# Adjacent weight rows per partition, d(o) as rows on four column groups, and four output buffers in a decode layer's forward and backward

## The chip, the cores and the metric

The kernel runs on one core of a Trainium2 chip. The metric is the device time of one execution in microseconds, the median of several runs. The time before is 290.5 us (five runs, 288.19 to 291.11 us).

## The reference

One decode step of a parallel layer: with `xn = layernorm(x)`, the output is `x + attention(xn) + ffn(xn)`, and all gradients for a given `grad_out` are returned too. There are 4 batch rows of one token, D = 512, 32 query heads in 8 key/value groups, head size 128, a cache of 4096 positions of which the last 1024 are attended, and a feed-forward width of 1792. Everything is bfloat16.

```python
def _A_ref(x, k_cache, v_cache, wq, wo):      # Hq 32, Hkv 8, Dh 128, W = 1024, rep = 4
    q = (x @ wq).reshape(B, Sq, Hq, Dh).transpose(0, 2, 1, 3)
    k = jnp.repeat(k_cache[:, :, Sk - W:, :], rep, axis=1)
    v = jnp.repeat(v_cache[:, :, Sk - W:, :], rep, axis=1)
    p = softmax(einsum("bhqd,bhkd->bhqk", q, k) * Dh ** -0.5)
    o = einsum("bhqk,bhkd->bhqd", p, v)
    return o.transpose(0, 2, 1, 3).reshape(B, Sq, Hq * Dh) @ wo

def _B_ref(x, w_gate, w_up, w_down):
    return (gelu(x @ w_gate) * (x @ w_up)) @ w_down

xn = layernorm(x)
out = x + _A_ref(xn, ...) + _B_ref(xn, ...)
# returned: out, and the gradients to x, k_cache, v_cache, wq, wo, w_gate, w_up, w_down
```

The gradients to the caches are 4 x 8 x 4096 x 128 each. They are zero outside the attended 1024 positions, and these zeros have to be written too: 50 MB of the 81 MB that the kernel writes.

## The kernel before

**Start and feed-forward.** x and grad_out are loaded with every batch row repeated on 32 partitions (`x_b`, `dy_b`, lines 110 to 114). The three feed-forward weights, the first two groups' wo and wq and most of their k and v are loaded on SP's queue. A weight matrix of 512 rows lies on 128 partitions as four chunks: partition p holds rows p, 128 + p, 256 + p and 384 + p (lines 118 to 122, 222), so each row is one contiguous run. `wo` has 1024 rows to a head group, laid out likewise as eight chunks of 128 rows of 1 KB (line 221). `xnT` and `dyT` (lines 204 to 210) are the normalized x and the gradient with D on the partitions, in the same chunk order. `xnm` and `dym` (lines 213 to 218) hold the rows masked by `msk_i`, so that partition b*32 + i keeps only row i of its block of 32: an outer product with a tile that has head i on that partition picks this head.

The feed-forward part (lines 516 to 659) transposes weights on TensorE (PE), evacuates them with `evac` (line 84) and multiplies them. `evac` gives a PSUM tile to ScalarE (ACT, line 92) or VectorE (DVE, line 94) by an estimate of the load on each; 16-bit tiles go to DVE. The weight gradients are appended as pieces to a list `bg`, and `tick(n)` runs n of them between other matmuls.

**Attention.** Eight key/value groups are taken two at a time, so t runs over 4 head groups of 8 heads each. For each t:

- `pre(t)` (line 280): wo is transposed (line 288), d(o) = wo dy is formed by matmuls of 4 columns (line 293) and q = wq xn likewise (line 298), both into one PSUM tile `doq_ps`. They are copied to `doT` and `qsT` (lines 305 and 307), from there into the zero-padded operands `dom` and `qm` (line 308; two sets, by the parity of t), and transposed to rows `r4` (line 313).
- `masks` (line 318), `scores` (line 327; k for q, then v for d(o), transposed block by block at line 336 and multiplied at line 341 in four column groups of 32), `softmax`, `softmax_d`.
- `odq(t, 0)` and `odq(t, 1)` (line 408): o = p v and dq = ds k, copied from PSUM to rows (lines 421 and 423), which two transposes (line 426) turn into columns (line 428).
- `pre(t + 1)` stands between the two `odq`.
- `fin(t)` (line 497): the products with wo and with the transposed wq are added into `acc`.
- `load_next(t)` (line 242): the loads for t + 2.
- `dw(t)` (line 455) appends the pieces of d(wo) (`piece_o`, line 463) and d(wq) (`piece_q`, line 478); `dvdk` appends those of the cache gradients (line 444).

**Order and queues.** SP issues all loads, in the program's order (`manual_schedule` for that engine alone); the other engines' instructions are placed by a scheduler that keeps to the data flow. GpSimd (POOL) issues the result stores through `store` (line 98). The zeros go out on ACT's queue at fixed points of the program (`zeros(n)`, line 253): each is tied behind the last ACT evacuation recorded then. At the end everything left of the zeros is issued (line 689).

**Pools.** Results wait for their store in `osb_*` tiles from the pool `outp` (line 75, three buffers, 4 KB to a partition) and `stg_*` tiles from `stage` (line 662, three buffers, 8 KB). Each t fills four osb tiles (two `osb_o`, two `osb_q`) and four stg tiles. `stage` and the tiles of odd groups (`wodd`) take the memory that the feed-forward pools gave back (line 661).

**The end** (lines 692 to 721): `acc` is transposed, and the layer norm's backward runs on DVE on 128 x 512 tiles.

Of the kernel before, what the change touches and what calls it, by code (L numbers as in the profile page):

```python
# [14 lines left out]
P = 128  # L15
# [3 lines left out]
def kernel(  # L19
# [23 lines left out]

    nc = tc.nc
# [21 lines left out]
    assert Sq == 1 and Dh == P and D == 512 and F % P == 0 and RG == 32 and JQ * NQ == J and WQ == JQ * P  # L66
# [8 lines left out]
    outp = ctx.enter_context(tc.tile_pool(name="outp", bufs=3))  # L75
# [44 lines left out]
    nc.sync.dma_start(out=wg_sb[:], in_=B_w_gate.rearrange("(c p) f -> p c f", p=P))  # L120
    wu_sb = ffn_w.tile([P, ND, F], BF16, name="wu_sb")
    nc.sync.dma_start(out=wu_sb[:], in_=B_w_up.rearrange("(c p) f -> p c f", p=P))
# [39 lines left out]
    qm_all, dom_all = [], []  # L162
    for i in range(2):
        for lst, nm in ((qm_all, "qm"), (dom_all, "dom")):
            t_ = const.tile([P, NS, RG + rep], BF16, name=f"{nm}{i}")
            nc.gpsimd.memset(t_[:], 0.0)
            lst.append(t_)
# [38 lines left out]
    for src, dstT in ((dy_b, dyT), (xn_b, xnT)):  # L206
        tps = ps_x.tile([P, ND, P], BF16, name="tps", tag="x")
        for c in range(ND):
            nc.tensor.transpose(tps[:, c, :], src[:, c * P:(c + 1) * P], ident[:])
        nc.vector.tensor_copy(out=dstT[:], in_=tps[:].rearrange("p c (b r) -> p c b r", b=B)[:, :, :, 0])  # L210


    xnm = const.tile([P, rep, D], BF16, name="xnm")
    dym = const.tile([P, rep, D], BF16, name="dym")
# [6 lines left out]
    wo_v = A_wo.rearrange("(t h p) n -> t p h n", p=P, h=HG)  # L221
    wq_v = A_wq.rearrange("(c p) (t j) -> t p c j", p=P, j=CW)
# [50 lines left out]
    def tick(n):  # L273
        for _ in range(min(n, len(bg))):
            bg.popleft()()
# [4 lines left out]
    def pre(t):  # L280

        wo_sb, wq_sb = wo_t[t], wq_t[t]
        dq_ps = ps_x.tile([P, 2, HG, B], FP32, name="doq_ps", tag="x")
        for h2 in range(HG // 2):
# [6 lines left out]
            for i in range(2):  # L291
                for c in range(ND):
                    nc.tensor.matmul(dq_ps[:, 0, 2 * h2 + i, :], lhsT=woT[:, i, c, :], rhs=dyT[:, c, :],
                                     start=(c == 0), stop=(c == ND - 1))
            tick(2)
        for h in range(HG):
            for c in range(ND):
                nc.tensor.matmul(dq_ps[:, 1, h, :], lhsT=wq_sb[:, c, h * Dh:(h + 1) * Dh], rhs=xnT[:, c, :],
                                 start=(c == 0), stop=(c == ND - 1))
        T4 = []  # L300
# [451 lines left out]
```

## Time and profile before

| | |
|---|---|
| median of 5 runs | 290.5 us (288.19 to 291.11) |
| profiled execution: its own time / its span | 288.19 us / 286.5 us |
| busy: PE, DVE, ACT, POOL | 207.5, 144.8, 113.8, 66.9 us (72, 51, 40, 23% of the span) |
| mean granted TensorE clock | 0.85 |
| memory traffic | 112.4 MB, mean 392 GB/s; read 30.93 MB, written 81.01 MB |
| landing times (median): wo, wq, kb, vb loads | 10.1, 16.1, 20.0, 48.8 us |
| landing times (median): stg_dv, stg_dk, osb_o, osb_q stores | 10.0, 9.4, 14.1, 12.6 us |
| landing times (median): zeros of 3 MB, of 1.5 MB | 16.4, 15.5 us |

The span runs from the first to the last instruction on the core, and the execution's own time is 1.7 us longer. The page divides the span into 40 equal slices; a digit is the busy share of a slice in tenths. An instruction's "mean ns of one" is its latency; matmuls overlap, so a row of them takes less than their sum. "Idle before" is the time that an engine stood still ahead of such instructions, with what released it. The three busy DMA queues are q1 (SP's loads), q10 (ACT's, here the zeros) and q0 (GpSimd's stores).

### The profile page before, as it was taken

To read this page: it belongs to the slowest core of one execution; us is meant where nothing else is said; L and a number is where in the kernel's file an instruction comes from. 1 tells how busy PE (TensorE), PEld (TensorE's weight loads), DVE (VectorE), ACT (ScalarE), POOL (GpSimd) and SP (SyncE) were. 2 spreads that over 40 slices of the span, in tenths; PEclk is the share of its full clock that TensorE was granted. 3 is DMA by queue.
4 is the path that set the end of the run, shared out by engine and by line. 5 is a ranking of instruction groups with operands and counts; after the bars stand their busy time and mean duration, and the time that the engine had idled before them with its cause. 6 is when DMAs were issued, how large, how long until landed. Compare 5 with 4: busy or idle time off the path is not lost.

```text
span 286.5 us, 6811 instructions
## 1 busy us (share of the span) xinstructions
PE 207.5 (72%) x2946; PEld 142.1 (50%) x2956; DVE 144.8 (51%) x310; ACT 113.8 (40%) x217; POOL 66.9 (23%) x84
## 2 busy tenths in 40 slices
PE   1397994973977899556699987576898688596810
PEld 0386882652644765333357655343575365362310
DVE  5484672333564567313636763145375535455770
ACT  1201654443442467313325653043455444245610
POOL 7000130431303152311033322112162231302410
PEclk9996999597897889795959996959799979869775
DMA  6999999999999999999999999999999999999897
GB/s 169 385 386 380 386 400 419 413 404 431 431 415 431 412 373 388 432 416 422 421 421 344 316 410 423 423 424 418 424 411 396 392 392 414 411 407 377 305 387 287
DMA packets 30181, 112.38 MB, mean 392 GB/s; under 512 B 1536, under 2 KB 7688, under 8 KB 26056
## 3 DMA queue, kind: packets, MB, share of 16 engines
q10 hardware_dynamic: 4612, 50.46, 42.0%
q1 hardware_dynamic: 17732, 30.81, 29.5%
q0 software_dynamic: 7808, 30.67, 27.4%
q8 instruction: 23, 0.38, 0.5%
q14 instruction: 6, 0.05, 0.0%
HBM read 30.93 MB, written 81.01 MB: 391 GB/s over the span
## 4 chain that ended last, share of the span: by engine, by line
PE 47%; DMA 28%; DVE 14%; issue 4%; ACT 3%; POOL 1%; SPq 0%; DVEq 0%; ACTq 0%; POOLq 0%
DMA out_dram<-osb_o 14%; PE T_ps L336 9%; PE kv_ps L444 7%; DMA out_dram<-stg_dv 5%; PE S_ps L341 4%; DVE T_sb L94 4%; DMA wd_sb<-in_B_w_down_dram 4%; PE od_ps L416 3%; DMA out_dram<-osb_d 3%; PE woT_ps L288 3%; PE acc_ps L181 2%; DMA out_dram<-osb_g 2%; PE wgT_ps L648 2%; PE wqT_ps L508 2%; PE dwo_ps L463 2%
## 5 line engine op out<-in xcount | busy, mean ns | idle before, releaser
L94 DVE COPY T_sb<-T_ps 128x1024 bf16<-128x1024 bf16 x64 | 44.2, 691 | 34.7 <-PE T_ps L336 34.3
L92 ACT CAST stg_dv<-kv_ps 128x512 bf16<-128x512 f32 x52 | 28.8, 589 | 43.9 <-PE kv_ps L444 40.9
L92 ACT CAST stg_dk<-kv_ps 128x512 bf16<-128x512 f32 x46 | 25.0, 588 | 15.4 <-PE kv_ps L444 7.6
L336 PE MATMUL T_ps<-ident,vb 128*128 128x128 bf16 x256 | 26.8, 255 | 4.8 <-DVE osb_q L94 4.8
L336 PEld LDWEIGHTS <-vb 128*128 128x128 bf16 x256 | 20.6, 116 | 11.1 <-issue 7.2
L336 PE MATMUL T_ps<-ident,kb 128*128 128x128 bf16 x256 | 24.4, 228 | 0.6 <-ACT stg_dk L92 0.2
L336 PEld LDWEIGHTS <-kb 128*128 128x128 bf16 x256 | 18.2, 102 | 12.3 <-issue 4.9
L92 ACT CAST osb_q<-dwq_ps 128x512 bf16<-128x512 f32 x25 | 13.5, 589 | 27.1 <-DMA out_dram<-osb_o 17.1
L444 PE MATMUL kv_ps<-domr,P_q 128*128 128x512 bf16 x63 | 23.7, 435 | 0.2 <-issue 0.2
L92 ACT CAST osb_g<-dwg_ps 128x384 bf16<-128x384 f32 (+1 forms) x30 | 14.5, 534 | 17.6 <-PE dwg_ps L621 6.4
L444 PE MATMUL kv_ps<-qmr,dS_q 128*128 128x512 bf16 x59 | 18.7, 391 | 3.2 <-ACT stg_dk L92 2.4
L94 DVE COPY woT<-woT_ps 128x1024 bf16<-128x1024 bf16 x16 | 11.1, 692 | 17.9 <-PE woT_ps L288 17.9
L478 PE MATMUL dwq_ps<-od_r,xnm 128*128 128x256 bf16 x64 | 13.1, 334 | 6.0 <-DVE osb_q L94 5.8
L92 ACT CAST osb_o<-dwo_ps 128x512 bf16<-128x512 f32 x23 | 12.8, 588 | 7.8 <-PE dwo_ps L463 7.8
L352 POOL TENSOR_TENSOR dS_q<-dS_b,qmsk 128x1024 bf16<-128x1024 bf16 x4 | 7.5, 1884 | 35.3 <-DVE dS_b L405 35.3
L94 DVE CAST stg_dk<-kv_ps 128x512 bf16<-128x512 f32 x18 | 12.0, 685 | 3.5 <-DMA out_dram<-stg_dv 2.5
L341 PE MATMUL S_ps<-T_sb,dom 128*32 128x256 bf16 x128 | 10.5, 312 | 4.4 <-DVE T_sb L94 4.3
L98 POOL DMA_DIRECT2D out_dram<-stg_dv x8 | 6.2, 774 | 30.9 <-ACT stg_dv L92 30.9
L98 POOL DMA_DIRECT2D out_dram<-osb_q x8 | 5.9, 732 | 31.4 <-ACT osb_q L92 31.3
L94 DVE COPY wqT<-wqT_ps 128x1024 bf16<-128x1024 bf16 x16 | 11.0, 688 | 4.2 <-PE wqT_ps L508 3.9
L288 PE MATMUL woT_ps<-ident,wo_sb 128*128 128x128 bf16 x128 | 12.2, 246 | 0.7 <-ACT osb_g L92 0.5
L94 DVE COPY wgT<-wgT_ps 128x1024 bf16<-128x1024 bf16 x14 | 9.7, 692 | 5.4 <-PE wgT_ps L648 5.4
(187 smaller groups left out, 374.3 us busy)
## 6 DMA issues: line engine op xcount, KB each, us to landing
out_dram<-ztile ACTq DMA_DIRECT2D x8, 3072.0 KB, 16.4
out_dram<-ztile ACTq DMA_DIRECT2D x16, 1536.0 KB, 15.5
kb<-in_A_k_cache_dram SPq DMA_DIRECT2D x8, 1024.0 KB, 20.0
vb<-in_A_v_cache_dram SPq DMA_DIRECT2D x8, 1024.0 KB, 48.8
out_dram<-stg_dv POOLq DMA_DIRECT2D x8, 1024.0 KB, 10.0
out_dram<-stg_dk POOLq DMA_DIRECT2D x8, 1024.0 KB, 9.4
wo_sb<-in_A_wo_dram SPq DMA_DIRECT2D x4, 1024.0 KB, 10.1
wq_sb<-in_A_wq_dram SPq DMA_DIRECT2D x4, 1024.0 KB, 16.1
```

Of the source, the lines that this page charges most:

```text
L92: last.append(nc.scalar.copy(out=out, in_=in_))
L94: return nc.vector.tensor_copy(out=out, in_=in_)
L98: d = eng.dma_start(out=out, in_=in_)
L181: nc.tensor.matmul(ps[:, c, :], lhsT=lf(c), rhs=rhs, start=(k == 0), stop=(k == len(terms) - 1))
L288: nc.tensor.transpose(wT_ps[:, i, c, :], wo_sb[:, 2 * h2 + i, c * P:(c + 1) * P], ident[:])
L336: nc.tensor.transpose(T_ps[:, j, :], blks[(t, g)][:, b, j, :], ident[:])
L341: nc.tensor.matmul(ps[q * RG:(q + 1) * RG, :], lhsT=lf[:, s * RG:(s + 1) * RG], rhs=T_sb[:, q * WQ:(q + 1) * WQ], start=(g == 0 and b == 0 ...
L352: nc.gpsimd.tensor_tensor(out=dst[:], in0=src[:].unsqueeze(1).broadcast_to([P, NQ, WQ]), in1=qmsk[:].unsqueeze(2).broadcast_to([P, NQ, WQ] ...
L416: nc.tensor.matmul(od_ps[b * RB:b * RB + rep, k, g, :], lhsT=pT[:, jj, c0:c0 + rep], rhs=blks[(t, g)][:, b, j, :], start=(j == 0), stop=(j ...
L444: nc.tensor.matmul(mps[:].rearrange("p b d -> p (b d)"), lhsT=src[:, q, jj * P:(jj + 1) * P], rhs=mr[:, g].rearrange("p b d -> p (b d)"), ...
L463: nc.tensor.matmul(mps[:], lhsT=o_r[:, g, :], rhs=dym[:, i, :], start=True, stop=True)
L478: nc.tensor.matmul(mps[:, i].rearrange("p g d -> p (g d)"), lhsT=xnm[:, i2 * 2 + i, c * P:(c + 1) * P], rhs=dq_r[:].rearrange("p g d -> p ...
```

## The change

- The weights' rows are dealt to the partitions in runs of adjacent rows: partition p of a head group's wo holds rows 8p to 8p + 7, and of w_gate, w_up and wq rows 4p to 4p + 3. w_down keeps its layout. The gradients d(wo), d(wq), d(w_gate) and d(w_up) are stored in the same order, xn is transposed with a stride of 4 to match, and the final layer-norm steps read `acc` in that order.
- d(o) is formed as rows: the transposed wo is the moving operand, dy with 8 copies of each batch row (`dyT8`) the stationary one, on four column groups. One copy (`do_row`) and two transposes give the columns back. q keeps its way, in a tile of its own.
- `odq(t, 0)` writes o four times, once per masked head (`o_x`), in the order of the new rows; eight small matmuls with `qmsk` give the columns `oT`, and `piece_o` multiplies `o_x` with `dy_b`. `dym` is then needed by the feed-forward alone and moves to its pool.
- One set of `qm` and `dom` in place of two; four buffers in `outp` in place of three.

```diff
-    outp = ctx.enter_context(tc.tile_pool(name="outp", bufs=3))
+    outp = ctx.enter_context(tc.tile_pool(name="outp", bufs=4))
...
-    nc.sync.dma_start(out=wg_sb[:], in_=B_w_gate.rearrange("(c p) f -> p c f", p=P))
+    nc.sync.dma_start(out=wg_sb[:], in_=B_w_gate.rearrange("(p c) f -> p c f", p=P))
...
-    nc.sync.dma_start(out=wu_sb[:], in_=B_w_up.rearrange("(c p) f -> p c f", p=P))
+    nc.sync.dma_start(out=wu_sb[:], in_=B_w_up.rearrange("(p c) f -> p c f", p=P))
...
-    qm_all, dom_all = [], []
-    for i in range(2):
-        for lst, nm in ((qm_all, "qm"), (dom_all, "dom")):
-            t_ = const.tile([P, NS, RG + rep], BF16, name=f"{nm}{i}")
-            nc.gpsimd.memset(t_[:], 0.0)
-            lst.append(t_)
+    qm, dom = [const.tile([P, NS, RG + rep], BF16, name=nm) for nm in ("qm", "dom")]
+    for t_ in (qm, dom):
+        nc.gpsimd.memset(t_[:], 0.0)
...
-            nc.tensor.transpose(tps[:, c, :], src[:, c * P:(c + 1) * P], ident[:])
+            nc.tensor.transpose(tps[:, c, :], src[:, c:D:ND] if adj else src[:, c * P:(c + 1) * P], ident[:])
...
+            dyT8 = const.tile([P, ND, B * 8], BF16, name="dyT8")
+            nc.vector.tensor_copy(out=dyT8[:].rearrange("p c (b r) -> p c b r", b=B),
+                                  in_=tps[:].rearrange("p c (b r) -> p c b r", b=B)[:, :, :, 0:8])
...
-    dym = const.tile([P, rep, D], BF16, name="dym")
+    dym = ffn.tile([P, rep, D], BF16, name="dym")
...
-    wo_v = A_wo.rearrange("(t h p) n -> t p h n", p=P, h=HG)
-    wq_v = A_wq.rearrange("(c p) (t j) -> t p c j", p=P, j=CW)
+    wo_v = A_wo.rearrange("(t p k) n -> t p k n", p=P, k=HG)
+    wq_v = A_wq.rearrange("(p c) (t j) -> t p c j", p=P, j=CW)
...
     def pre(t):
-        dq_ps = ps_x.tile([P, 2, HG, B], FP32, name="doq_ps", tag="x")
+        E = P // HG
+        do_ps = ps_x.tile([P, HG, GP, E], FP32, name="do_ps", tag="x")
...
-            for i in range(2):
-                for c in range(ND):
-                    nc.tensor.matmul(dq_ps[:, 0, 2 * h2 + i, :], lhsT=woT[:, i, c, :], rhs=dyT[:, c, :],
-                                     start=(c == 0), stop=(c == ND - 1))
+            for c in range(ND):
+                for i in range(rep):
+                    nc.tensor.matmul(do_ps[i * RG:(i + 1) * RG, 2 * h2:2 * h2 + 2], lhsT=dyT8[:, c, :],
+                                     rhs=woT[:, :, c, :].rearrange("p j (g x) -> p j g x", g=GP)[
+                                         :, :, :, i * E:(i + 1) * E], start=(c == 0), stop=(c == ND - 1),
+                                     tile_position=(0, i * RG))
             tick(2)
+        do_row = attw.tile([P, GP * E, HG], BF16, name="do_row", tag="do_row", bufs=1)
+        nc.vector.tensor_copy(out=do_row[:], in_=do_ps[:].rearrange("p k g e -> p (g e) k"))
+        dq_ps = ps_w.tile([P, HG, B], FP32, name="dq_ps", tag="w")
...
+        doT_ps = ps_x.tile([P, HG, B, 8], BF16, name="doT_ps", tag="x")
+        for g in range(GP):
+            nc.tensor.transpose(doT_ps[:, g * rep:(g + 1) * rep].rearrange("p i b r -> p (i b r)"),
+                                do_row[:, g * E:(g + 1) * E, :].rearrange("p e k -> p (e k)"), ident[:])
...
     def odq(t, k):
...
         if k == 0:
-            nc.vector.tensor_copy(out=rows[:], in_=od_ps[:, k])
...
+            X = attw.tile([P, HG, GP, rep, P // HG], BF16, name="o_x", tag="o_x", bufs=1)
+            for i in range(rep):
+                src = od_ps[:, 0].rearrange("p g (e k) -> p k g e", k=HG)
+                if i % 2:
+                    nc.scalar.activation(out=X[:, :, :, i, :], in_=src, func=ACT.Copy, scale=msk_i[:, i:i + 1])
+                else:
+                    nc.vector.tensor_scalar(out=X[:, :, :, i, :], in0=src, scalar1=msk_i[:, i:i + 1], scalar2=None,
+                                            op0=ALU.mult)
+            X = X[:].rearrange("p k g i e -> p k (g i e)")
+            oT_ps = ps_w.tile([P, HG, B], FP32, name="oT_ps", tag="w")
+            for h in range(HG):
+                nc.tensor.matmul(oT_ps[:, h, :], lhsT=X[:, h, :], rhs=qmsk[:], start=True, stop=True)
+            oT = attw.tile([P, HG, B], BF16, name="oT", tag="oT")
+            nc.vector.tensor_copy(out=oT[:], in_=oT_ps[:])
...
         def piece_o(g, i, held):
-            nc.tensor.matmul(mps[:], lhsT=o_r[:, g, :], rhs=dym[:, i, :], start=True, stop=True)
+            nc.tensor.matmul(mps[:], lhsT=X[:, g * rep + i, :], rhs=dy_b[:], start=True, stop=True)
...
-                r0 = (t * HG + g * rep) * Dh
-                store(nc.gpsimd, out=out_5[r0:r0 + rep * Dh, :].rearrange("(h p) n -> p h n", p=P),
-                                    in_=held["osb"][:], kind="rest",
+                store(nc.gpsimd, out=out_5[t * CW:(t + 1) * CW, :].rearrange("(p k) n -> p k n", k=HG)[
+                    :, g * rep:(g + 1) * rep, :], in_=held["osb"][:], kind="rest",
...
-                                 lhsT=xnm[:, i2 * 2 + i, c * P:(c + 1) * P],
+                                 lhsT=xnm[:, i2 * 2 + i, c:D:ND],
...
-            store(nc.gpsimd, out=og[c * P:(c + 1) * P, :],
+            store(nc.gpsimd, out=og.rearrange("(p c) f -> p c f", c=ND)[:, c, :],
...
-        nc.vector.reduce_sum(out=s1[:], in_=acc_d, axis=AX.X)
+        nc.vector.reduce_sum(out=s1[:], in_=acc_d, axis=AX.XY)
```

## The prediction

> **What bounds the kernel now.** I read the page's slices first: they tell whether an engine or the memory traffic is full.
>
> ```profile
> PE   1397994973977899556699987576898688596810
> PEclk9996999597897889795959996959799979869775
> DMA  6999999999999999999999999999999999999897
> GB/s 169 385 386 380 386 400 419 413 404 431 431 415 431 412 373 388 432 416 422 421 421 344 316 410 423 423 424 418 424 411 396 392 392 414 411 407 377 305 387 287
> DMA packets 30181, 112.38 MB, mean 392 GB/s; under 512 B 1536, under 2 KB 7688, under 8 KB 26056
> q10 hardware_dynamic: 4612, 50.46, 42.0%
> q1 hardware_dynamic: 17732, 30.81, 29.5%
> q0 software_dynamic: 7808, 30.67, 27.4%
> ```
>
> PE goes up and down; the DMA row stands at 9 nearly everywhere, and q10 (the zeros), q1 (the loads) and q0 (the result stores) add up to 98.9% of 16 engines. The transfers are the bound. But a busy engine moves anything from 305 to 432 GB/s, so I took the rate by stretches:
>
> ```profile
> 98.00:110.00 12.00, 11.76 (x144) 8.16 (x141) 8.32 (x18) 7.17 (x14) 4.53 (x3) 0.86 1.01 370
> 110.00:150.00 40.00, 27.50 (x340) 17.31 (x340) 16.23 (x34) 13.47 (x27) 8.25 (x8) 0.79 1.02 422
> 150.00:166.00 16.00, 15.36 (x250) 10.97 (x253) 11.28 (x23) 9.40 (x19) 5.28 (x4) 1.00 0.98 335
> 166.00:210.00 44.00, 32.45 (x453) 21.37 (x452) 19.04 (x41) 15.84 (x31) 9.00 (x9) 0.81 1.02 422
> 210.00:222.00 12.00, 10.89 (x140) 7.19 (x139) 8.37 (x16) 7.01 (x13) 5.28 (x4) 1.00 0.99 399
> 222.00:262.00 40.00, 31.47 (x421) 20.52 (x421) 20.53 (x42) 17.69 (x34) 8.63 (x9) 0.87 1.01 401
> 262.00:274.00 12.00, 6.98 (x29) 3.10 (x29) 7.31 (x12) 6.86 (x13) 3.56 (x5) 0.86 0.87 324
> ```
>
> Columns: stretch, its length, PE, PEld, DVE, ACT, POOL busy, granted clock, DMA share, GB/s. Two kinds of stretch alternate. At 422 GB/s PE is busy 27.5 of 40 us, so compute waits for the memory. At 370, 335 and 399 PE is full (15.36 of 16) and the memory is underfed: no zero stores are pending there, and they are issued only when ACT gets further. The chain of waits says what compute waits for in the full stretches:
>
> ```profile
> 113.09 17.24 DMA out_dram<-osb_o
> 168.75 18.28 DMA out_dram<-osb_o
> 249.40 14.05 DMA out_dram<-stg_dv
> ```
>
> The fourth osb tile of a head group waits for the first to land, as the pool has three.
>
> **The change, part by part.** All sums are made against the profiled execution: span 286.5, time 288.19 us. The median of the five runs is 290.5, 0.8% above it.
>
> *Larger runs in the loads.* The page gives q10 as 4612 packets, 50.46 MB, 42.0% of 16 x 286.5 = 1925 us of engine time, and q1 as 17732, 30.81 MB, 1352 us. Taken as a cost per packet plus a cost per MB, the two rows give 11.8 ns per packet and 37.1 us per MB. The third row tests it: q0 comes to 7808 x 0.0118 + 30.67 x 37.1 = 1230 us, and its 27.4% is 1256. The 7688 packets under 2 KB are the 4096 rows of wo, 1792 of w_down, 256 of x and dy, 1536 tiny ones and 8 output rows: so q1 has one packet per row. After the change wo has 4 x 128 runs of 8 KB for 4 x 1024 rows of 1 KB (3584 packets fewer), w_gate and w_up 256 runs of 14 KB for 1024 rows (768 fewer). 4352 x 11.8 ns = 51 us, over 16 engines **3.2 us**. If runs were cut at the 3.9 KB that a q0 packet has on average, wo would keep 1024 packets and the gates would gain nothing: 3072 x 11.8 / 16 = 2.3. q10's packets average 10.9 KB, so a hardware queue does carry long ones, and I take 3.2. The wq load keeps its 2 KB runs: nothing.
>
> The Trainium skill's page "DMA: Bandwidth & Descriptors", section "Specifications", speaks against this term: it puts the smallest transfer for line rate at 512 B. By it 1 KB rows are full rate already and the term is 0, not 3.2. The trace leans the other way: a stretch in which the 1 KB rows of a wo load travel, 158 to 162 us, shows 316 GB/s at a DMA share of 1.03.
>
> *Larger runs in the stores of dwo.* The 7688 small packets are all accounted for by loads, so q0 joins 1 KB rows into long packets already. I take 0. Bounds: 8 stores x 384 fewer rows x 11.8 ns / 16 = 2.3 us gain if the rows cost as in q1; and no loss, since osb_q is already written as separate pieces and lands in 12.6 us where osb_o takes 14.1.
>
> *Four osb buffers.* The fourth tile no longer waits: the 17.2 and 18.3 us leave the chain. The transfers are full there (422 GB/s), so this is no gain by itself. What is late next is the following head group's k and v loads, the three stg buffers (the 14.05 us row) and the zeros. What it buys is that compute arrives at its heavy stretches earlier, with zeros still pending. What underfeeding costs now, against 422 GB/s: 12 x (1 - 370/422) = 1.5, 16 x (1 - 335/422) = 3.3, 12 x (1 - 399/422) = 0.7; and at the end, against the 401 of a stretch that only stores, 12 x (1 - 324/401) = 2.3. Together 7.8. Two wo loads lie in the first two, and 2 x 3584/4 x 11.8 / 16 = 1.3 of it is counted above: 6.5 left. Bounds: 6.5 if all fills up, 0 if the starved stretches only move. I take half, **3.2**: the end should mend, since osb_q waits 2.4 us there for osb_o while zeros are still to be issued, but each loss of pending zeros has its own point in the program. Against it: loads that finish earlier leave a longer stretch of stores alone at 401; 15 us of that cost 15 x 21/422 = **0.7**.
>
> *do as rows.* Per head group 64 matmuls of 64 columns on four column groups replace 32 of 4. The 32 of line 298 ran in 0.80 to 0.94 us, 27 ns each; the four column-group matmuls of line 341 with 256 columns took 0.29. So 64 cost 1.7 (27 ns) to 4.6 us (16 groups at 0.29) in place of 4 x 0.35 for line 293. With short columns I take the lower end: +0.3. Two transposes add 2 x 0.27 (line 313) and do_row a copy of 0.42 (DVE, 128x256 from PSUM, line 421). PE waits for do_row behind the 32 q matmuls placed before the transposes, 0.8 us, which cover it. o_x is four copies for one: +0.42 DVE, +0.78 ACT (line 423: 0.39). Eight narrow matmuls, 0.2, replace two transposes. Sum per head group: PE +0.9 (upper end 3.8), DVE +0.8, ACT +0.8. The masked xn rows become weights with every fourth column (xnm at lines 478 and 621, 96 loads): the only strided weight load in the trace, 4 columns of aT_b at line 598, takes 105 ns, and contiguous ones 97 to 119, so 0; at double the time, 96 x 0.11 = 10.6 us over the whole run, under the same cover. The cover is the 14 to 18 us that compute waits per head group. If it is gone, because the memory starves in just that stretch, it costs 4 x 0.9 = 3.6 (upper 15). I take 0.
>
> The skill's "TensorEngine Tiling (Array Packing)", section "Key Properties", says that changing the tiling mode drains the array, and the change puts eight more such switches in each head group. The trace has such switches already, around every score matmul:
>
> ```profile
> 162.57 0.13 PEld L341 LDWEIGHTS <-qm 128*32 128x32 bf16 x4
> 162.60 0.29 PE L341 MATMUL S_ps<-T_sb,qm 128*32 128x256 bf16 x4
> 162.82 0.10 PEld L336 LDWEIGHTS <-kb 128*128 128x128 bf16 x1
> ```
>
> The full-width weight load starts 0.07 us before the column-group matmuls end, so no drain shows. By 0.07 us a switch the rule would cost 8 x 4 x 0.07 = 2.2 us of PE, under the same cover.
>
> *Edits at nothing.* One qm and dom: pre's writes come after both score passes of the previous group on PE, in program order. One o_x: its eight piece_o readers run within the next group's k scores, before odq writes it again. dym in the FFN pool: its last reader is line 609, and the last osb_d store leaves at 41.78; the loads of group 1 that reuse the pool queue on SP from 40.68, are needed some 50 us later, and only they stand behind it. Strided reads in the last DVE steps: these end at 278.7, the last zeros land at 285.0. POOL loses two memsets; its stores keep their order.
>
> Sum: 288.2 - 3.2 - 3.2 + 0.7 = 282.5; at the ratio of median to profile, 1.008, **284.8 us**.
>
> **The rivals.**
> *A, forecast:* less packet work and better-fed transfers. For it: DMA share 98.9%, waits on osb. 284.8; its own range, 281.4 with everything recovered (288.2 - 3.2 - 6.5 + 0.7 = 279.2, x 1.008) to 288.2 with packets alone at 2.3 (285.9 x 1.008). Chance 0.70.
> *B, the buffers buy nothing and the rows little:* the stalls come back as waits for k/v loads or stg buffers, and the 1 KB rows cost less than the fit says. For it: loads of v take 48.8 us to land, so compute that runs ahead meets them. Between 0 and 2.3 us of gain at the profile: 288.1 to 290.5, middle 289.3. Chance 0.16.
> *C, slower, PE sets the pace:* the starved stretches are where the new PE work stands (pre and fin; PE 15.36 of 16 busy). If zeros run out there as before, every microsecond of it counts. Place: 98 to 110, 150 to 166 and 210 to 222. Price: 3 x 3.8 = 11.4 at the upper end, less 3.2 for packets: 296.4, x 1.008 = 298.8. It decides once the column-group matmuls cost over (3.2 + 2.9) / 3 = 2 us per group and no stall is saved (2.9 is 1% of 290.5). Against it: 27 ns neighbours. Typical 295. Chance 0.10.
> *D, the change doesn't do what it says:* the runs are still cut into rows. Without 3.2 the forecast gives 285.7, x 1.008 = 288.0. Chance 0.04.
>
> **How the numbers follow.** This kernel's runs spread over 1%, so 1% is what can be told from no change. Faster by over 1% (below 287.6): nearly all of A and a part of D, 0.70. Slower by over 1% (above 293.4): C, and a bad edge of B, where new waits cost more than the rows give, 0.12. The rest, 0.18. The range is A's low end less a margin for the 2.3 of the dwo stores, 280, up to 291, where B is in and C left out.
>
> **What would show it.** Right: q1 near 13400 packets and below 28.5%; "under 2 KB" near 3600; no wait of osb_q on osb_o; 150 to 166 and the last 20 us above 390 GB/s. Wrong: new chain pieces on kb, vb or stg of over 10 us; PE full and DMA under 370 GB/s in longer stretches than before; column-group matmuls that take over 0.2 us per four; q1's share unchanged with fewer packets.

## The result, and the profile after

The changed kernel takes 290.44 us (median of 45 runs, 288.65 to 292.53), the kernel before, run beside it, 290.37 (87 runs). The ratio is 1.0014, 95% interval 0.9999 to 1.0028: no change that can be told. The forecast was 284.8. Here and below a ratio leaves out the runs that were disturbed by the chip's slower state and a median does not, so the two can differ, and no line of a disturbed run's profile is used.

The profiled execution after has a span of 289.7 us and a time of its own of 291.38, 0.9 above its median; that of before was 2.2 below its median. So some 3 us of what the two pages differ by is the spread of the runs and nothing of the change. From the page of the kernel after, the slices and the three large queues:

```profile
PE   0397998758877995977889688303998679598700
ACT  3001665544523573552336444004445435337700
DMA  4999999999999999999999999999956999999995
GB/s 134 401 415 386 385 395 413 424 372 428 422 424 416 424 413 423 424 421 423 418 411 401 412 428 421 422 416 398 416 200 273 391 406 387 402 415 361 365 412 222
DMA packets 25830, 112.39 MB, mean 388 GB/s; under 512 B 1536, under 2 KB 3592, under 8 KB 20936
q10 hardware_dynamic: 4612, 50.46, 41.5%
q1 hardware_dynamic: 13380, 30.81, 28.2%
q0 software_dynamic: 7808, 30.67, 26.7%
```

Two things are to be seen. The packets came as forecast (13380 in q1, 3592 under 2 KB). And the DMA row, which before held its 9 to the last slice but two, has a 5 and a 6 from 210 us on, above 200 and 273 GB/s; PE and ACT show 3, 0 and 0, 0 ahead of it, from 181 to 195 us.

These rows allow an account that the prediction should have made. A queue's share times the span is the time that its packets took on 16 engines. Before, 98.9% of 286.5 is 283.3 us of packets and 3.2 us in which engines stood free. After, 96.4% of 289.7 is 279.3 us of packets and 10.4 us free. **The change saved 4.0 us of packets and left the engines free for 7.2 us more.** Beside the 3 us of spread, the second eats up the first. The account is rough: it nets out stretches whose share is shown as 1.02 or 1.03, it leaves out a small fourth queue (0.5%), and it stands on one execution of each kernel.

The same stretches as in the prediction, of the kernel after (PE, PEld, DVE, ACT, POOL busy, granted clock, DMA share, GB/s):

```profile
98.00:110.00 12.00, 11.27 (x147) 7.15 (x145) 8.52 (x14) 8.32 (x16) 2.10 (x3) 1.00 1.01 413
150.00:166.00 16.00, 13.46 (x160) 8.33 (x158) 10.55 (x19) 8.10 (x16) 2.09 (x3) 0.97 1.03 405
166.00:210.00 44.00, 23.07 (x378) 15.74 (x380) 14.69 (x29) 12.91 (x27) 6.61 (x6) 0.73 1.02 417
210.00:222.00 12.00, 11.91 (x185) 8.88 (x183) 7.92 (x19) 6.31 (x12) 5.28 (x4) 0.86 0.51 194
262.00:274.00 12.00, 9.70 (x68) 4.60 (x66) 10.57 (x18) 9.96 (x19) 4.09 (x6) 1.00 0.93 355
```

The stretches that I had called underfed rose from 370 to 413 and from 335 to 405 GB/s, as forecast, and the time did not move. The first of them did so at the same share, 1.01: other packets went through the same busy engines. From 210 to 222 the rate fell from 399 to 194 at a DMA share of 0.51: here the engines really stand free, for 5.9 us. PE is busy 11.91 of 12 us there, after 23.07 of 44 in the stretch ahead: it is catching up on something. The chain of waits, and ScalarE's rows of the timeline around it, name it:

```profile
48.78 11.42 DMA out_dram<-osb_g
...
153.97 43.38 DMA kb<-in_A_k_cache_dram
197.37 0.61 ACTq L100
198.02 2.05 ACT stg_dv L94 x4
...
253.88 12.34 DMA out_dram<-stg_dv
```

```profile
186.36 11.62 ACTq L100 DMA_DIRECT2D out_dram<-ztile  x2
198.02 2.05 ACT L94 CAST stg_dv<-kv_ps 128x512 bf16<-128x512 f32 x4 [17.61 <-DMA kb<-in_A_k_cache_dram]
```

Both waits for osb_o (17.24 and 18.28 us before) are gone. In their place stands a k load: issued at 153.97, landed at 197.35. It is not its data that is missed. ScalarE waits for it ahead of *issuing two stores of zeros*, and its evacuations stand in line behind them: the waits view says what that did to PE.

```profile
ACT stg_dv L94 <- DMA kb<-in_A_k_cache_dram: 17.6, 1, 17.6
PE pT_ps L376 <- ACT stg_dv L94: 14.5, 1, 14.5
```

Before, the longest waits of ScalarE for a transfer were for an osb store, and none was for a load:

```profile
ACT osb_q L92 <- DMA out_dram<-osb_o: 17.1, 3, 8.1
```

A store of zeros needs no load. The compiled program shows the tie: every transfer of SyncE and ScalarE reports on one of eight completion semaphores, dealt out in turn over both queues, and a transfer waits until the last one on its semaphore has landed. The first of these two zero stores waits for semaphore DMAHW2, the second for DMAHW3.

These had last gone to wq and the first k load of group 3. Those loads are slow *because* zeros are pending. From 170 to 185 us the trace has 335 packets of zeros (12 KB), 334 of result stores (4 KB) and 359 of loads (2 KB): the queues take turns packet by packet, which left the loads 49 of 416 GB/s. In the kernel before, no zeros travel from 150.3 to 171.2 us, and wo, wq and the first k load of group 3 go through in that gap, to 170.6 us. In the kernel after, the gap ends at 167.1 us and that k load's packets begin at 165.8.

So the theory to test: the packets' time is shorter; compute has more to do in each head group and no cover for it; the fourth buffer pays for that; and the zeros that are now issued earlier wait for loads on shared semaphores, hold ScalarE, and leave a hole in the transfers.

### The profile page after: what moved, and what is told of

The parts are those of the page before. It is cut to its first block, busy times and chain, and to the rows that moved or that the text cites. A ratio compares the mean times of both kernels' runs of the same rounds, so it can differ in the third digit from the quotient of the medians.

```text
span 289.7 us, 7133 instructions
## 1 busy us (share of the span) xinstructions
PE 205.5 (71%) x3102; PEld 143.1 (49%) x3116; DVE 149.8 (52%) x319; ACT 116.7 (40%) x225; POOL 64.6 (22%) x82
## 2 busy tenths in 40 slices
DMA packets 25830, 112.39 MB, mean 388 GB/s; under 512 B 1536, under 2 KB 3592, under 8 KB 20936
## 3 DMA queue, kind: packets, MB, share of 16 engines
q1 hardware_dynamic: 13380, 30.81, 28.2%
q0 software_dynamic: 7808, 30.67, 26.7%
## 4 chain that ended last, share of the span: by engine, by line
PE 46%; DMA 27%; DVE 14%; issue 5%; ACT 4%; SPq 0%; ACTq 0%; DVEq 0%
DMA kb<-in_A_k_cache_dram 15%; PE T_ps L351 8%; PE kv_ps L474 6%; DMA out_dram<-stg_dv 4%; DMA out_dram<-osb_g 4%; DVE T_sb L96 4%; PE woT_ps L294 4%; PE S_ps L356 4%; DMA wd_sb<-in_B_w_down_dram 4%; PE wgT_ps L677 3%; PE wqT_ps L537 3%; PE dwq_ps L507 2%; PE acc_ps L180 2%; PE wdT_ps L565 2%; PE od_ps L431 2%
## 5 line engine op out<-in xcount | busy, mean ns | idle before, releaser
L351 PE MATMUL T_ps<-ident,vb 128*128 128x128 bf16 x256 | 26.0, 247 | 0.5 <-DVE osb_q L96 0.3
L351 PE MATMUL T_ps<-ident,kb 128*128 128x128 bf16 x256 | 23.3, 220 | 0.9 <-ACT osb_g L94 0.3
L351 PEld LDWEIGHTS <-kb 128*128 128x128 bf16 x256 | 17.2, 97 | 10.9 <-issue 3.4
L474 PE MATMUL kv_ps<-domr,P_q 128*128 128x512 bf16 x60 | 22.2, 428 | 0.4 <-issue 0.4
L474 PE MATMUL kv_ps<-qmr,dS_q 128*128 128x512 bf16 x59 | 20.1, 417 | 1.4 <-ACT stg_dk L94 0.6
L537 PEld LDWEIGHTS <-wq_sb 128*128 128x128 bf16 x128 | 11.5, 123 | 6.9 <-issue 5.9
L537 PE MATMUL wqT_ps<-ident,wq_sb 128*128 128x128 bf16 x128 | 13.4, 265 | 1.6 <-issue 1.6
L376 PE MATMUL pT_ps<-ident,dS_b 128*128 128x128 bf16 x8 | 1.2, 240 | 18.2 <-ACT stg_dv L94 14.5
L100 POOL DMA_DIRECT2D out_dram<-stg_dk x8 | 6.1, 768 | 33.6 <-ACT stg_dk L94 14.1
L294 PE MATMUL woT_ps<-ident,wo_sb 128*128 128x128 bf16 x128 | 13.4, 254 | 0.0
## 6 DMA issues: line engine op xcount, KB each, us to landing
wo_sb<-in_A_wo_dram SPq DMA_DIRECT2D x4, 1024.0 KB, 12.8
```

Source lines behind the costliest of these rows:

```text
L100: d = eng.dma_start(out=out, in_=in_)
L294: nc.tensor.transpose(wT_ps[:, i, c, :], wo_sb[:, 2 * h2 + i, c * P:(c + 1) * P], ident[:])
L351: nc.tensor.transpose(T_ps[:, j, :], blks[(t, g)][:, b, j, :], ident[:])
L474: nc.tensor.matmul(mps[:].rearrange("p b d -> p (b d)"), lhsT=src[:, q, jj * P:(jj + 1) * P], rhs=mr[:, g].rearrange("p b d -> p (b d)"), ...
L537: nc.tensor.transpose(wT_ps[:, i, c, :], wq_sb[:, c, h * Dh:(h + 1) * Dh], ident[:])
```

## The experiments

Every ratio is against runs of the kernel before on the same chip, with its 95% interval. "Packets" and "free" are the account above, from each page (three shares times the span, and the rest of it).

| kernel | median us | ratio | packets / free us |
|---|---|---|---|
| before | 290.37 | 1 | 283.3 / 3.2 |
| after | 290.44 | 1.0014 (0.9999 to 1.0028) | 279.3 / 10.4 |
| after, three osb buffers | 299.08 | 1.0176 (1.0093 to 1.0258) | 281.8 / 10.2 |
| after, zero rows of 6 KB | 290.66 | 0.9895 (0.9849 to 0.9942) | |
| after, do matmuls twice | 293.05 | 1.0105 (1.0045 to 1.0165) | 278.9 / 12.2 |
| after, whole zero stores | 288.34 | 0.9908 (0.9871 to 0.9946) | 278.1 / 8.6 |
| before, all runs of rows | 293.76 | 1.0122 (1.0039 to 1.0205) | 282.6 / 10.6 |
| before, four osb buffers | 290.65 | 0.9992 (0.9951 to 1.0033) | 282.1 / 8.1 |
| do and o as rows alone | 295.39 | 1.0104 (1.0013 to 1.0194) | |
| before, four osb, whole zero stores | 288.64 | 0.9955 (0.9916 to 0.9995) | 281.0 / 6.6 |
| after, zeros on SyncE | 289.29 | 0.9964 (0.9934 to 0.9995) | 278.5 / 9.2 |
| before, runs of wo alone | 293.44 | 1.0083 (1.0037 to 1.0128) | 281.7 / 8.4 |
| before, order of wq alone | 292.71 | 1.0074 (1.0036 to 1.0113) | |
| before, whole zero stores | 288.48 | 0.9967 (0.9934 to 0.9999) | 282.8 / 3.7 |
| after, zeros on SyncE, whole | 289.29 | 0.9960 (0.9934 to 0.9987) | 279.4 / 8.0 |
| after, zeros on SyncE, 6 KB rows | 290.37 | 1.0015 (0.9975 to 1.0056) | 282.4 / 6.4 |
| after, last zeros on ScalarE, rest on SyncE | 290.85 | 1.0011 (0.9976 to 1.0046) | 278.4 / 9.8 |

Where no profile is used the last column is empty. The ratios of the kernel after with three osb buffers and of d(o) and o as rows alone rest on three runs each, that of all runs of rows on five. A single profiled execution lies up to 2 us from its kernel's median (with three osb buffers 5 us below it), so differences of 1 or 2 us in the last column say little.

**The fourth buffer taken away from the kernel after.**

```diff
-    outp = ctx.enter_context(tc.tile_pool(name="outp", bufs=4))
+    outp = ctx.enter_context(tc.tile_pool(name="outp", bufs=3))
```

> The changed kernel with three osb buffers again. Theory R (the run-ahead): the larger runs save 2.8 us of every DMA engine's time, and the fourth buffer gives this back, because compute that runs ahead keeps zeros pending all the time, the loads of group 3 crawl, and ACT then stands 16 us behind zero stores that wait for two of those loads. With three buffers compute waits for osb stores as before, ACT's idle time before zero stores stays under 3 us in the profile, no stretch of 4 us after 200 us and before 260 us falls under 300 GB/s, and the time is 0.5 to 1.5% below the kernel before (286 to 289 us). Rival P (the new PE work sets the pace): with a buffer less, nothing covers it; the time is equal to or up to 1% above the changed kernel, 290.4 to 293 us. Rival N (the runs save nothing and the buffer does nothing): 290 to 291 us with q1's share at 28%.

1.0176. The theory that the fourth buffer gives back what the rows gained fell: without it the change is slower, by more than any of the three theories had, and the buffer is worth 1.6% *to this kernel*. The chain of this run has the old waits back, a little longer than before:

```profile
40.06 9.76 DMA out_dram<-osb_d
...
117.19 18.87 DMA out_dram<-osb_o
...
174.25 18.82 DMA out_dram<-osb_o
```

Before they stood at 40.05, 113.09 and 168.75. The first osb_o wait begins 4.1 us later: 1.9 had built up by the end of the feed-forward's waits, the other 2.2 lie in the head group. They are not all new compute: with the rows' order alone, without d(o) as rows, the same stretch is 1.2 us longer (runs of rows alone, below). The wait behind it did not get shorter by that, it got longer, and the delay is carried to the second (5.5 us later). That is the first crack in the step "the cover is the 14 to 18 us that compute waits": a wait for a store that begins when compute is done looks as if in series with it.

**Zeros from 128 partitions in rows of 6 KB (kernel after).** A finer packet of zeros should let loads through faster.

```diff
-    ZP = P // 2
+    ZP = P
```

> The changed kernel with the zeros written from 128 partitions in rows of 6 KB instead of 64 partitions in rows of 12 KB. The number and size of the zero stores, and where they are issued, stay. Theory R says that the queues take turns by packets, so a load beside pending zeros moves 2 KB for every 12 KB of zeros: with 6 KB the loads should get about 1.5 to 2 times their 48 GB/s beside zeros, group 3's kb should land by 185 us instead of 197, ACT's wait before zero stores shrinks from 16 us to under 6, and the time falls to 285 to 289 us although 4096 more packets cost 3 us by the fit of the page. Rival P: no change beyond the packets' cost, 290 to 293.5 us. Rival N: 293 us, the cost of the packets alone.

The ratio is 0.9895, but the median of all 12 runs, 290.66, says no change: five lie between 286.07 and 288.93, seven between 290.52 and 292.82. Nothing is built on it.

**The column-group matmuls of d(o) done twice (kernel after).**

```diff
-            for c in range(ND):
+            for c in [c_ for _ in range(2) for c_ in range(ND)]:
```

> The changed kernel with the matmuls that form d(o) on four column groups run twice (the second pass overwrites the first with the same values). Theory R: PE has slack where these stand, 256 more matmuls at the 25 to 30 ns each that the changed profile shows cost 7 us of PE and under 1.5 us of time, 290 to 292 us. Rival P: PE sets the pace in these stretches, so the time rises by most of 7 us, 295 to 298 us.

1.0105 against 1.0014: 0.9%, or 2.6 us, for 256 more matmuls, between the two expectations. They are as cheap as forecast; the group view of the kernel after has, with busy time, mean ns and the idle time before:

```profile
L299 PE MATMUL do_ps<-woT,dyT 128*32 128x64 bf16 x256 | 5.3, 206 | 1.9 <-DVE woT L96 1.9
L440 ACT ACTIVATE o_x<-od_ps,msk_i 128x256 bf16<-128x256 f32 x8 | 3.9, 488 | 0.7 <-DVE o_x L442 0.7
```

256 of them keep PE busy for 5.3 us, 1.3 per head group. Yet doubling them costs 2.6 us of the run. Work that was priced at nothing, as lying under a wait, reaches the time at about half its own length. (In this kernel the waits for osb_o are gone, so it does not test that cover itself.)

**Whole zero stores (kernel after).** The zeros that open the second region are issued four at once, which turns 24 stores into 18 with the same bytes, and so moves which store meets which semaphore.

```diff
-            zeros(2 if t == 0 else 0)
+            zeros(4 if t == 0 else 0)
```

> The changed kernel with four blocks of zeros instead of two after the first group's k scores. All later zero stores of groups 0, 1 and most of 2 and 3 then come as one store of 3 MB instead of two of 1.5 MB, so there are 18 zero stores instead of 24, and they fall on other completion semaphores: the third and later zero store of a group no longer stands behind the kb loads. Theory R (with the semaphore as the thing that holds ACT): ACT's longest wait before a zero store is under 4 us, the stretch from 208 to 222 us keeps above 350 GB/s, and the time falls to 284 to 288 us. If it is not the semaphore but the slow loads themselves that hold compute (PE waits for kb or vb in their place), the time stays within 1% of the changed kernel and the chain shows PE behind a load. Rival P: no change, 290 to 291 us.

0.9908: 0.9% faster than the kernel before (interval 0.5 to 1.3%), with the lowest median of all. The stretches of this run:

```profile
166.00:210.00 44.00, 31.55 (x490) 22.14 (x493) 20.46 (x44) 16.79 (x34) 11.05 (x9) 0.81 1.02 421
210.00:222.00 12.00, 7.72 (x90) 4.99 (x88) 4.11 (x8) 3.81 (x8) 1.07 (x2) 0.86 0.99 370
262.00:274.00 12.00, 9.51 (x51) 4.24 (x49) 8.66 (x15) 8.13 (x15) 3.37 (x5) 0.86 0.73 276
```

The hole at 210 to 222 is gone (share 0.99 for 0.51), and PE did 31.55 us of work in the stretch ahead for 23.07. One long ScalarE wait on a load is left, and the last stretch gives a part back (share 0.73):

```profile
ACT stg_dv L94 <- DMA wq_sb<-in_A_wq_dram: 13.2, 1, 13.2
```

So a wait of this kind does not always leave a hole of this size; what the edit changed is which load is waited for, and when.

**Runs of rows alone, on the kernel before.** All loads and stores in the new order, nothing else; the weights' rows then meet the vectors of other rows.

```diff
-    wo_v = A_wo.rearrange("(t h p) n -> t p h n", p=P, h=HG)
-    wq_v = A_wq.rearrange("(c p) (t j) -> t p c j", p=P, j=CW)
+    wo_v = A_wo.rearrange("(t p k) n -> t p k n", p=P, k=HG)
+    wq_v = A_wq.rearrange("(p c) (t j) -> t p c j", p=P, j=CW)
...
```

> The kernel before with the larger runs alone: all loads and stores of wo, wq, w_gate, w_up and their gradients in the new row order, three osb buffers, d(o) in columns as before. Its multiplications then pair wrong rows, so its output differs from the reference; the amount of work is that of the kernel before. Theory S (in series): three osb buffers with the change cost 1.8% because the wait for an osb store is a fixed store time in series with compute and covers nothing, so new PE work in pre lengthens every group, while the larger runs save what the page's fit says where traffic is full, and nothing where the queue is starved. It expects 0 to -1% here, 287.5 to 290.5 us. Rival W (the new row order is slower in memory: in the three-osb run the wq rows of groups 2 and 3 took 127 and 134 ns against 96 and 107): 292 to 297 us here, and no change in the run with d(o) as rows alone.

1.0122: the part that I had counted as the sure gain makes the kernel *slower* when it comes alone. The packets do take less (282.6 for 283.3), but 10.6 us are free for 3.2. The chain shows the first place: osb_d waits 12.06 us where it waited 8.89, and osb_o 19.88 and 18.97. Of the two theories Rival W has the time.

**The fourth buffer alone, on the kernel before** (with one set of qm and dom, and single P_q and dS_q, to make room).

```diff
-    outp = ctx.enter_context(tc.tile_pool(name="outp", bufs=3))
+    outp = ctx.enter_context(tc.tile_pool(name="outp", bufs=4))
...
```

> The kernel before with four osb buffers alone (one set of qm and dom, and one buffer for the quartered P and dS, make the room). Theory S: the two waits of 17 to 18 us for osb_o leave the chain, zeros stay pending through pre and fin, and the time falls by 1 to 2.5%, 283 to 287.5 us, unless ACT gets stuck behind loads as in the changed kernel; then 288 to 290. Rival F (traffic is full, so the buffers give nothing by themselves): within 0.3%, 289.5 to 291.5 us.

0.9992: nothing, as Rival F expected. But the reason is not that traffic is full. Its chain and its waits on loads:

```profile
92.00 37.69 DMA wo_sb<-in_A_wo_dram
...
158.57 48.08 DMA kb<-in_A_k_cache_dram
```

```profile
ACT stg_dv L92 <- DMA kb<-in_A_k_cache_dram: 22.4, 2, 12.7
ACT osb_q L92 <- DMA wo_sb<-in_A_wo_dram: 12.1, 1, 12.1
```

The same mechanism, without any of the new rows: 34.5 us of ScalarE behind loads, one of them a wo load in 1 KB rows that took 37.69 us. The stretch 210 to 222 has 217 GB/s at a share of 0.55. Theory S had named this case, at 288 to 290 us. In the kernel after, wo lands in 12.8 us and this wait is missing, which fits that the rows and the buffer help each other; no run tests it alone. Over all profiles used, the kernels with three buffers show no ScalarE wait on a load, and those with four and zeros on ScalarE show 13 to 35 us of it.

**d(o) and o as rows alone** (the kernel after with the old order of rows and three buffers; here too the rows meet others than they should).

> The changed kernel with the old row order in all loads and stores and three osb buffers: d(o) as rows, o written four times, one set of qm and dom, alone. Its multiplications then pair wrong rows, so its output differs from the reference; the amount of work is that of the changed kernel. Theory S: about 2 us per head group on the path between the last pending zeros and the next, 3 to 4 times: 294 to 299 us. Rival W: 290 to 291.5 us.

1.0104, about 3 us for work of which I had priced 3.6 and taken 0. Rival W, which had the time of the runs of rows alone, expected no change here, so neither theory holds in both.

**Four buffers and whole zero stores, on the kernel before.**

> The kernel before with four osb buffers and the zeros in whole stores of 3 MB (four blocks after the first group's k scores), without larger runs and without d(o) as rows. Theory S: what four buffers give and what the whole zero stores give (1% on the changed kernel) both stay, 281 to 285 us, faster than either kernel. Rival F: as the changed kernel with whole zero stores, 288 us, because the time is then set by the traffic alone, plus 2 to 3 us for the rows of 1 KB.

0.9955 against 0.9992 with the buffer alone: in the direction of the theory, but the intervals overlap. The free time falls from 8.1 to 6.6 us. The waits are not gone: ScalarE still stands 22.5 us behind wo loads, 210 to 222 us is full (422 GB/s), and the hole lies at 232 to 244 us, with 215 GB/s at a share of 0.52.

**Zeros on SyncE (kernel after).** The same stores at the same points of the program, behind the same evacuations, so that SyncE does the waiting.

```diff
-            z = store(nc.scalar, og[b, g:g + w, 0:K0, :].rearrange("g (m j) d -> m g (j d)", m=ZP), zsrc, "zeros",
-                      ["rest", "zeros"])
+            z = store(nc.sync, og[b, g:g + w, 0:K0, :].rearrange("g (m j) d -> m g (j d)", m=ZP), zsrc, "zeros",
+                      ["rest"])
...
-                              mybir.DependencyInfo(mybir.DependencyClass.NoSync, mybir.DependencyReason.DATA))
+                              mybir.DependencyInfo(mybir.DependencyClass.Sync, mybir.DependencyReason.DATA))
```

> The kernel after, with every zero store issued by SyncE in place of ScalarE, at the same points of the program and behind the same ScalarE evacuation. Zeros and loads still take the same eight completion semaphores in turn, but ScalarE's evacuations no longer stand behind a zero that waits for a load. Theory S (in the kernel after ScalarE's 17 us of waits behind loads make the starved stretch at 210 to 222 us): no ScalarE wait on a load or a zero is left, the stretch around 210 to 222 us has over 350 GB/s in place of 194, and the time is 286 to 289, ratio to the kernel before 0.985 to 0.995. Rival T (the hole comes from the transfers themselves, the wait only reports it): a stretch of under 250 GB/s stays somewhere between 190 and 230 us, ratio 0.998 to 1.01. Both know that loads and zeros now share one queue, so a load may stand behind a zero store of 3 MB (7 to 8 us): that would show as new waits for wo, wq or k loads and could cost up to 3%.

The slices of this run:

```profile
PE   1397999849697986969895978997796930081000
DMA  4999999999999999999999999999999999999970
GB/s 127 403 412 383 387 405 428 409 415 410 427 420 423 428 390 413 396 410 428 421 427 411 400 409 405 388 426 413 426 407 414 414 407 421 415 405 392 419 279 15
```

No ScalarE wait on a load is left, 210 to 222 us moves 409 GB/s, and PE is done at 261 us. With the waits the hole went, so the hole came from ScalarE's waits. But the time is 0.9964, just outside what was expected, because the end is now empty: from 278 us the DMA share is 0.32, then under 0.1, while the last packets trickle out for 6 us. The packet records tell what they are: from 279.5 to 284.5 us exactly one packet is under way at any time, with the share at 0.06 to 0.07, which is one engine of 16. Each transfer reports its completion in sixteen steps: of the last store 15 came by 279.7 us and the sixteenth at 285.1.

**Which of the rows' loads costs.** Two halves of the run with all runs of rows: the wo lines alone, and the wq lines alone (the rows of wo, or of wq, again meet other rows).

> The kernel before, with only wo's rows dealt to the partitions in runs of eight (its load, 8 KB runs, and the store of its gradient); the rows are then paired wrongly. All four changes of row order together had cost 1.2% on the kernel before. Theory W (long load packets take longer turns against the stores, and wo in 8 KB lands early so that the load queue runs empty): ratio 1.006 to 1.012, the waits for osb_o at or over 18 us. Theory Q (wq's new order is what costs): ratio 0.99 to 1.002, as 3584 packets fewer are the whole packet gain of my forecast (2.6 of 3.2 us).

> The kernel before, with only wq's rows dealt in runs of four adjacent rows (its load and the store of its gradient; packets stay at 2 KB, neighbours on a partition now lie 8 KB apart in memory in place of 1 MB); the rows are then paired wrongly. Theory W: ratio 0.997 to 1.003, the 2 KB packets of wq at 96 to 107 ns as in the kernel before. Theory Q: ratio 1.006 to 1.012, the packets of wq at 125 ns and more, 150 to 166 us at 330 GB/s or less.

1.0083 and 1.0074: both cost, and neither of the two theories has it alone. For wo the chain shows how:

```profile
39.90 10.11 DMA out_dram<-osb_d
...
59.70 7.17 DMA out_dram<-osb_g
...
115.82 18.44 DMA out_dram<-osb_o
...
172.51 18.03 DMA out_dram<-osb_o
```

osb_d waits 10.11 for 8.89 and osb_g 7.17 for 6.75, as the next loads run beside the stores of the feed-forward part: the packets of wq(1) start at 49.1 us for 55.4. Later the opposite: these loads are done at 86.6 us for 96.9, wo(2) is issued at 101.0 for 98.3 and brings its first packet at 104.4, and the load queue is empty for 17.8 us where it was for 3.7. 98 to 110 us has a share of 0.92 and 330 GB/s, 150 to 166 one of 0.88 and 326. Why wq's order costs 0.7% at the same packet sizes stays open.

**Whole zero stores alone, on the kernel before.**

> The kernel before with the zero stores cut as in the run with whole zero stores (18 stores of 3 MB and 1.5 MB in place of 24), nothing else: three osb buffers, old rows. With four buffers the same edit gave 0.4 to 1.1%. Theory S (it takes the ScalarE waits behind loads away, which the kernel before does not have, as its longer waits for osb_o let the loads land first): ratio 0.998 to 1.005. Rival U (fewer and larger zero stores are simply better, or move zeros to where they are wanted): ratio 0.988 to 0.995.

0.9967, between the two expectations: the edit gives 0.3% even where no ScalarE wait of this kind stands, and 1.1% on the kernel after. The rest may belong to the waits, but the intervals are wide, and on the kernel before with four buffers, which has such waits, the edit gave 0.4%.

**Three versions with the zeros on SyncE:** whole stores, rows of 6 KB, and the last three of eight regions back on ScalarE.

> The kernel after with all zeros on SyncE and cut as whole stores (18 in place of 24). With the zeros on SyncE no hole was left before 262 us, but 8.8 us of unused transfer time stood in the last stretch: from 278 to 285 us the share of the transfer engines was 0.02 to 0.3, a few packets of 12 KB and then 4 KB at a time, as if one of the 16 engines had its own backlog to finish. Theory S (the packets of the changed kernel need 280 us of 16 engines, and what is lost beyond that is holes): if the end has 4 us of unused time as the kernel before has, the time is 284 to 286, ratio 0.978 to 0.985. Theory V (an always full kernel pays for one engine's backlog, however the zeros are cut): 288 to 290, the share under 0.3 for the last 5 us again.

> The kernel after with all zeros on SyncE and written from 128 partitions in rows of 6 KB in place of 64 in rows of 12 KB. Short rows had added 2.6 us of packet time with the zeros on ScalarE (122.7 against 120.1 us). Theory V' (the backlog comes from rows of 12 KB on 64 partitions, dealt unevenly to the engines): the last 5 us fill up, 284 to 287, ratio 0.98 to 0.988. Theory V (backlog of one engine in any case): 289 to 292.

> The kernel after with the first five of eight zero regions on SyncE and the last three on ScalarE, each behind the same evacuation. The zeros of groups 0 to 2 then don't hold ScalarE, and the last ones run beside the loads' queue rather than in it. Theory S: no ScalarE wait of over 2 us on a load before 222 us, and the end as in the kernel before (about 4 us unused): 284 to 287, ratio 0.978 to 0.988. Rival: the last zeros wait on completion semaphores that zeros on SyncE hold, ScalarE stands again for 5 to 10 us, and the time is 288 to 291.

289.29, 290.37 and 290.85 us: none comes near 285. In the first two the transfers are full to some 277 and 280 us and then run dry for 6 us; with 6 KB rows only the place of the tail moves. In the third ScalarE waits again ahead of zeros (2.43 and 5.46 us), then 18.00 us for a stg_dv store until 263.93, and the stretch 262 to 274 falls to 186 GB/s:

```profile
262.00:274.00 12.00, 7.77 (x36) 4.06 (x35) 8.03 (x13) 7.17 (x13) 3.32 (x5) 0.73 0.48 186
```

With 6 KB rows the tail is again one packet at a time, from 282.5 to 287 us; with whole stores it is four, then three, two and one. So a backlog of one engine, or of a few, is what the end waits for. Why these engines fall behind no run shows.

## Why the prediction was wrong

*Packets, -3.2 us: right as packet time, wrong as run time.* Counts are exact, q1 went from 84.5 to 81.7 us, all queues together from 283.3 to 279.3, 4.0 us. The packet records give 50.6 ns for 1 KB, 87 for 2 KB and 318 for 8 KB, so 1 KB in long rows costs 39.8 ns where it cost 50.6. The rule that the prediction took from the Trainium skill's "DMA: Bandwidth & Descriptors", section "Specifications" (line rate from 512 B), would make these equal; here the measurement decides against it. But these prices depend on what travels beside: the runs of rows alone took 282.6 us in all (8 KB at 332 ns, 2 KB at 90), 0.7 less than before, and the fourth buffer alone took 282.1 with the old rows. The step that failed first is the silent one from packet time to run time. Alone, the runs of rows made the kernel 1.2% slower where the sum had 3.2 us of gain: with wo's rows alone the loads disturb stores earlier (osb_d) and then leave their queue empty.

*Stores of dwo, 0: within its bounds.* q0 keeps 7808 packets and goes from 78.5 to 77.3 us.

*Four osb buffers, -3.2 (0 to 6.5): the step that failed by its reason.* It said "At 370, 335 and 399 PE is full and the memory is underfed". The rows that it quoted have DMA shares of 1.01, 0.98 and 0.99: the engines were occupied there with packets of 1 and 2 KB, and the low rate was their price, not free time. All free time before was some 3.2 us of the profiled span (98.9% of it was packets, a number that stands in the prediction), so 6.5 us could not be got by feeding. The stretches were filled as forecast and the time stayed. The term's other half was unseen: zeros that go out earlier meet loads on shared semaphores, and ScalarE stands 17.6 us. The kernel with the buffer alone (0.9992, 34.5 us behind loads) and the one with the zeros on SyncE (no wait on a load, no hole at 210 to 222 us) show it from two sides. That the buffer is worth 1.6% inside the change seems to have another reason than the one forecast: it makes up for what the rows cost.

*do as rows, "under the same cover ... I take 0": wrong in the cover, right in the price.* A head group's d(o) keeps PE busy 1.3 us, o_x takes 482 and 488 ns a copy (422 and 388 forecast), and total PE busy is 205.5 for 207.5 us. But the wait for osb_o is for a store that starts when compute is done, and with four buffers it is gone. Doubled matmuls cost 2.6 us, the rows alone 1.0%; where in the head group this time goes was not shown. The drain on a change of tiling that the skill's "TensorEngine Tiling (Array Packing)", section "Key Properties", has was not seen as a price: 16 of these matmuls ran in 0.30 to 0.52 us.

*Edits at nothing:* no run speaks against them.

*The rivals.* B is what happened in time (288.1 to 290.5, measured 290.4) and in form, "the stalls come back as waits for k/v loads"; it had a chance of 0.16. The forecast's own sign of being wrong came too, a chain piece on kb of over 10 us (43.38). B's reason was another one: compute does not miss the data, ScalarE is held by an issue. C did not come: the new PE work is cheap. D is excluded by the counts.

So the parts are: rows of d(o) +1.0%, runs of rows +1.2%, both together with three buffers +1.8%, and the fourth buffer -1.6% on top of them, but 0 alone. The nearest to the forecast's gain is the kernel after with whole zero stores, 288.34 us. Why even a kernel without the hole does not turn 4 us of saved packets into time is narrowed (the unused time goes to the end, to one or a few engines with a backlog) but not settled.

## What to carry to other kernels

Take a queue's packet time and the free time apart before calling a stretch starved: share times span is the first, and a low GB/s at a share of 1 is dear packets, which feeding cannot improve. A wait for a store that starts when compute ends may be no cover for new compute: ask what starts the store. And on an engine that both evacuates PSUM and issues transfers, list what each issue waits for, its completion semaphore included, before freeing it to issue earlier.

## What the runs showed of the hardware

Beside pending 12 KB zeros and 4 KB stores, loads of 2 KB packets get some 49 GB/s: the engines go by packets, not by bytes (335, 334 and 359 of them in 15 us), and a 1 MB k load landed 43 us after its issue. Its sixteen completion steps came from 170.9 to 197.4 us, so it waited for the last engine.

Nearly alone, the same packets take longer each: wq(2) and wq(3) had a mean of 96 and 107 ns in the kernel before, at 343 and 320 GB/s in all, and 84 in the kernel after, where result stores above all filled the engines beside them (424 and 412 GB/s in all).
